# Last batch's queries and keys turned by DMA instead of TensorE, and MLP groups that choose their PSUM bank

## The chip, the cores and the metric

The kernel runs on one core of one Trainium2 chip. The time is device microseconds from the launch of the program to its end on that core. Before the change ten runs gave a median of 292.9 us (291.88 to 293.35).

## What is computed

Two blocks follow each other. The first is chunked attention with a few memory rows: 4 batches, 8 heads, 768 positions, 64 dimensions, chunks of 32 queries.

```python
for c in range(nc):                       # 24 chunks
    q_c   = q[:, :, 32*c : 32*c + 32]
    k_ctx = k[:, :, max(0, 32*c - 16) : min(768, 32*c + 40)]
    v_ctx = v[:, :, same range]
    a = softmax(q_c @ concat(mem_k, k_ctx).T / 8)      # 8 memory rows
    out[:, :, 32*c : 32*c + 32] = a @ concat(mem_v, v_ctx)
```

The second takes the heads side by side as x (4, 768, 512), mixes it with a Fourier transform along positions and along channels, and applies an MLP:

```python
u  = x + real(fft(fft(x, axis=1), axis=2))
un = (u - mean(u)) / sqrt(var(u) + 1e-6)
out = u + relu(un @ w_ch1) @ w_ch2                     # 512 -> 2048 -> 512
```

Inputs and output are float32.

## The kernel before

The work is 16 attention steps (n = 0 to 15; each is a pair of heads of one batch, four steps per batch), then for each batch a Fourier stage and an MLP.

**One attention step.** `e_load_qk` (L321) loads the pair's queries and keys with a cast to bf16, one DMA each on GpSimd's queue: 96 partitions, on each of them 8 neighbouring positions of both heads (tiles qs and ks, three of each). `e_load_v` (L327) issues seven DMAs on SP. `e_turn_q` and `e_turn_k` (L354, L363) transpose on TensorE, 16 small transposes each (`turn`, L347, line L351 in the profile), into a PSUM tile trq or trk. ScalarE copies trq into qT with positions in order (`e_qT`, L360) and trk into the windows of kTb (`e_kT`, L379; for batch 0 VectorE does that). `e_scores` (L392) makes the scores of six 64-query blocks, 12 matmuls of 64 columns, twice per step; `e_exp` (L400) takes exponents on ScalarE; `e_values` (L416) multiplies by the values in fp32; `e_norm` (L426, L427) divides on VectorE into xsb.

**Fourier and MLP of a batch.** VectorE folds xsb, splits it into fp16 halves (hi on ScalarE, lo on VectorE), TensorE makes the row transform (ps, L488; batch 0: L627, L614) and the column transform (pm, L638, L539). The lower half of the positions needs mirrored rows: `e_rows_out` (L522, GpSimd's queue) writes them to DRAM, `e_rows_turn` (L526, SP) reverses them there, `e_mirror` (L531, GpSimd's queue) reads them back as xr. VectorE adds (L644, L546, L548) and takes statistics (L652); ScalarE subtracts the mean into un (L658). For batches 1 to 3 un is transposed by a DMA on SP (`e_flip`, L670) into unT; for batch 0 by TensorE. The MLP runs in two halves of 384 positions: 16 groups `e_ch1` (ph, L698, four matmuls of 384 columns), each followed by a ReLU on ScalarE (`e_relu`, L706, hT), then three blocks of `e_ch2` (pc, L713, sixteen matmuls of 512 columns) and `e_osb` (L720) on VectorE.

**PSUM.** Two banks are tagged acc (Fourier results, and batch 0's key turns), two mlp, one each tr and xa, two sc. An MLP group's tag is fixed by its index:

```python
def mtag(b, i):
    return "acc" if i % 3 == 2 else "mlp"
```

**What sets the order.** Nothing is scheduled at run time: every engine runs its instructions in a written order. `Plan` (L37) makes that order once, before the program is built. Each task has an engine, a cost, tasks that it follows (`after`, `behind`), buffer slots that it takes and gives, and a rank; `Plan.order` (L90) walks through time, starts on each engine the task of lowest rank that is ready, and lists the tasks in order of their start. MLP tasks have the highest ranks on TensorE and so fill what is left between the others. While TensorE waits early in batch 0, the plan writes in matmuls on zeros (`e_fill`, L771, idle in the profile). DMAs get a time on a shared queue model (`share`).

At the start GpSimd clears edges and tiles (L296, L754, L777), and then issues the loads of step 3 (line L324 in the profile).

Of the kernel before, what the change touches and what calls it, by code (L numbers as in the profile page):

```python
# [36 lines left out]
class Plan:  # L37
# [11 lines left out]
    def __init__(self, slots):  # L49
        self.free = dict(slots)  # L50
        self.tasks = []

    def add(self, engine, cost, emit, after=(), take=(), give=(), rank=None, moved=0.0,
            loose=False, late=0.0, filler=False, behind=None, lag=0.0):
        t = dict(engine=engine, cost=cost, emit=emit, after=[a for a in after if a is not None],
                 take=take, give=give, rank=len(self.tasks) if rank is None else rank,
                 moved=moved, done=None, at=None, no=len(self.tasks), loose=loose,
                 late=late, filler=filler, behind=behind, lag=lag)
        self.tasks.append(t)
        return t  # L60
# [29 lines left out]
    def order(self):  # L90
        now, idle = 0.0, {}
        self.flow, self.seen = {}, 0.0
        waiting = {}
# [6 lines left out]
        while any(waiting.values()):  # L100
            for tag in [g for g in gives if g[0] <= now]:
                gives.remove(tag)
                self.free[tag[1]] += 1
            moved = False
            for e, ts_ in waiting.items():
                if idle.get(e, 0.0) > now:
                    continue
                held = False
                for t in ts_:
                    slack = (self.SLACK if e == "PE" and now > self.FIRST and not t["filler"]  # L110
                             else 0.0)
                    if held and not t["loose"]:
                        continue
                    if any(a["done"] is None
                           or (a["end"] > now if a["engine"] == e else a["done"] > now - slack - t["lag"])
                           for a in t["after"]):
                        held = held or (e == "SP" and not t["loose"])
                        continue
                    if t["behind"] is not None and t["behind"]["at"] is None:
                        continue  # L120
                    need = {}
                    for tag in t["take"]:
                        need[tag] = need.get(tag, 0) + 1
                    if any(self.free[tag] < m for tag, m in need.items()):
                        held = held or (e == "SP" and not t["loose"])
                        continue
                    for tag in t["take"]:
                        self.free[tag] -= 1
                    cost = t["cost"] * (2.0 if e == "PE" and now < self.WARM else 1.0)
                    idle[e] = t["end"] = now + cost  # L130
                    if t["moved"]:
                        self.flow.setdefault(e, []).append([t, t["moved"], now + cost])
                        self.share(now)
                        t["end"] = t["done"]
                    else:
                        t["done"] = now + cost + self.LAG.get(e, 0.07)
                    for tag in t["give"]:
                        gives.append((t["done"], tag))
                    t["at"] = now
                    placed.append(t)  # L140
                    ts_.remove(t)
                    moved = True
                    break
                else:
                    if e == "PE" and self.filling and self.filling[0]["at"] is not None \
                            and self.filling[1]["at"] is None:
                        cost = self.FILL * (2.0 if now < self.WARM else 1.0)
                        idle[e] = now + cost
                        placed.append(dict(engine="PE", cost=cost, emit=self.fill, at=now,
                                           done=now + cost))  # L150
                        moved = True
# [12 lines left out]
def kernel(  # L164
# [61 lines left out]
    NKT = 2  # L226
    kTb = [spool.tile([P, NT, P], BF16, name=f"kTb{i}") for i in range(NKT)]

    cp_q = "p h j d -> p h (j d)"
# [3 lines left out]
    plan = Plan(dict(qs=NS, ks=NS, va=NV, kTb=NKT, qT=2, tr=1, sc=1, xa=1, e1=3,  # L233
# [87 lines left out]
    def e_load_qk(n, i):  # L321
        b, pr = seq[n]
        src, dst = ((q, qs), (k, ks))[i]
        nc.gpsimd.dma_start(dst[n % NS][0:QP],  # L324
                            src[b, 2 * pr:2 * pr + 2].rearrange("h (p j) d -> p h (j d)", j=RB))
# [27 lines left out]

    def e_turn_q(n):  # L354
# [22 lines left out]
    def e_kT(n, eng=None):  # L377
        trk = tr_of.pop((n, 1))
# [6 lines left out]
    def e_scores(n, g):  # L385
        qT, kT = qT_of[n], kTb[n % NKT]
        sc_of[n, g] = sc = aps.tile([P, 2, 8, 64], FP32, tag="sc", bufs=1, name="sc")
        for t6 in range(6):
            t = 6 * g + t6
            for hh in range(2):  # L390
                r0 = 64 * hh
                nc.tensor.matmul(sc[:, hh, t6, :], kT[r0:r0 + 64, t, :],  # L392
                                 qT[r0:r0 + 64, ts(t, 64)], start=True, stop=True,
# [296 lines left out]
    def mtag(b, i):  # L690
        return "acc" if i % 3 == 2 else "mlp"
# [3 lines left out]
    def e_ch1(b, sh, ht):  # L695
        ph_of[b, sh, ht] = ph = bank(mtag(b, ht), [P, 512], FP32, "ph")
# [12 lines left out]
    def e_ch2(b, sh, stl, part):  # L709
        if part == 0:  # L710
            pc_of[b, sh, stl] = bank(mtag(b, stl), [P, DM], FP32, "pc")
# [95 lines left out]
    t_gate, LATE = None, 1.0  # L807

    def attention(n):
# [3 lines left out]
        lq, lk = [add("POOL", 0.9, lambda i=i: e_load_qk(n, i), take=(("qs", "ks")[i],),  # L813
                      moved=1.2, late=LATE if b else 0.0,
                      behind=t_gate if n == HP else t_ck.get(n - 1),
# [6 lines left out]
        if n == HP - 1:  # L822
            def e_gate():
# [3 lines left out]
        tq = add("PE", 0.40, lambda: e_turn_q(n), [lq, t_idb], take=("tr",), give=("qs",))  # L827
        dve = ("DVE", nc.vector.tensor_copy) if n < HP else ("ACT", None)
        eq = add("ACT", 0.80, lambda: e_qT(n), [tq], take=("qT",), give=("tr",),
                 rank=SINES - 0.5 if n == 0 else None)  # L830
        ktag = "acc" if first else "tr"
        tk = add("PE", 0.43, lambda: e_turn_k(n), [lk, t_idb, t_kz if n == 0 else t_kzs], take=(ktag,), give=("ks",))
        mk = t_mk[n] = add("DVE", 0.2, lambda: e_mkT(n), [t_mkT, t_kTz[n % NKT], t_mk.get(n - 1)],
                           take=("kTb",))
        ek = add(dve[0], 1.25 if dve[1] else 1.04, lambda: e_kT(n, dve[1]), [tk, mk], give=(ktag,))
# [157 lines left out]
    def columns_of(b, t_rest):  # L993
# [25 lines left out]
        for i, kt in enumerate(kts):  # L1019
# [14 lines left out]
            if b > 0:  # L1034
                t_un[kt] = add("SP", 0.1, lambda kt=kt: e_flip(b, kt),
                               [un, t_un.get(kts[i - 1]) if i else None],
                               take=("unT",) if i == 0 else (), give=("un",), moved=0.8,
# [11 lines left out]
    def mlp(b, t_un, rs):  # L1049
        for sh in range(2):  # L1050
            relu = []
            c2 = None
            for ht in range(NHT):
                ph = add("PE", 0.65, lambda sh=sh, ht=ht: e_ch1(b, sh, ht),
                         mlp_prev + [t_un[slot(b, 3 * sh + i)] for i in range(3)] + t_w1,
                         take=(mtag(b, ht),), give=("unT",) if sh == 1 and ht == NHT - 1 else (),
# [3 lines left out]
                                take=("hT",) if ht == 0 else (), give=(mtag(b, ht),),  # L1060
                                rank=RELU(len(plan.tasks))))
            for stl in range(3):
                st, end_b = slot(b, 3 * sh + stl), 3 * sh + stl == NST - 1
                for part in range(4):
                    end = part == 3
                    c2 = add("PE", 0.88, lambda sh=sh, stl=stl, part=part: e_ch2(b, sh, stl, part),
                             [relu[4 * part + 3], t_w2[part], c2], take=(mtag(b, stl),) if part == 0 else (),
# [4 lines left out]
                          give=(mtag(b, stl), "xsb") if end_b else (mtag(b, stl),),  # L1072
# [62 lines left out]
```

## Time and profile before

| | us |
|---|---|
| median of ten runs (lowest, highest) | 292.9 (291.88, 293.35) |
| the profiled execution, its own time | 291.95 |
| its span, first to last instruction | 290.2 |
| TensorE busy | 273.6 |
| VectorE busy / ScalarE busy | 164.6 / 164.6 |
| GpSimd busy | 48.2 |

The granted TensorE clock is 0.998 over the span. PE is TensorE, DVE VectorE, ACT ScalarE, POOL GpSimd, SP the engine that issues most DMAs. Matmuls are pipelined: a matmul's duration in the profile overlaps the next one's, so the cost of a group is read from start to start. The chain that ended last follows the program back from its last instruction, at each step to what released it.

| stretch (us) | PE busy | ACT busy | DVE busy | DMA GB/s |
|---|---|---|---|---|
| 0 to 10 | 2.45 | 6.87 | 8.44 | 131 |
| 22 to 40 | 18.00 of 18 | 9.91 | 17.34 | 190 |
| 100 to 120 | 20.00 of 20 | 15.27 | 13.78 | 145 |
| 120 to 140 | 20.00 of 20 | 16.07 | 14.62 | 172 |
| 200 to 220 | 19.11 of 20 | 10.03 | 9.82 | 66 |
| 260 to 280 | 20.00 of 20 | 7.84 | 2.25 | 66 |

### The profile page before, as it was taken

How to read it: one execution, taken by the hardware profiler on the slowest of the kernel's cores; microseconds unless marked ns; L12 is line 12 of the kernel's file. 1: busy time of each engine (PE TensorE's matmuls, PEld its weight loads, DVE VectorE, ACT ScalarE, POOL GpSimd, SP SyncE). 2: the span in 40 equal slices, each digit the busy share in tenths (PEclk: the TensorE clock that was granted, in tenths of full speed). 3: DMA queues.
4: the chain of work that ended last, by engine and by line, in shares of the span. 5: the costliest groups of instructions: out<-in, count | busy, mean ns of one | idle time of the engine just before them, and what ended most of it. 6: DMA issues, size and time to landing. Idle time of an engine off the chain costs nothing.

```text
span 290.2 us, 7349 instructions
## 1 busy us (share of the span) xinstructions
PE 273.6 (94%) x3055; PEld 172.6 (59%) x3055; DVE 164.6 (57%) x354; ACT 164.6 (57%) x294; POOL 48.2 (17%) x96
## 2 busy tenths in 40 slices
PE   1489998999999999999999999999899999999994
PEld 1377797765566766566677656656554645545541
DVE  7879998951269865948884978864912012012011
ACT  5897456768566586877884257433750721712700
POOL 8823922310321010221010021000020000000000
PEclk9999999999999999999999999999999999999999
DMA  6999999997999995899940366954222504004204
GB/s 104 200 188 161 206 210 196 196 198 146 193 201 267 165 258 69 137 134 230 164 100 29 38 145 183 147 145 111 54 54 82 101 10 125 13 36 108 38 36 108
DMA packets 98689, 38.36 MB, mean 132 GB/s; under 512 B 85728, under 2 KB 93920, under 8 KB 98656
## 3 DMA queue, kind: packets, MB, share of 16 engines
q1 hardware_dynamic: 87344, 21.83, 40.5%
q0 software_dynamic: 10592, 15.21, 27.6%
q10 hardware_dynamic: 720, 0.85, 0.9%
q8 instruction: 24, 0.39, 0.6%
q14 instruction: 9, 0.07, 0.1%
HBM read 37.36 MB, written 13.37 MB: 175 GB/s over the span
## 4 chain that ended last, share of the span: by engine, by line
PE 88%; DVE 4%; POOL 4%; ACT 2%; issue 1%; POOLq 0%; DVEq 0%
PE pc L713 29%; PE ph L698 29%; PE xa L416 8%; PE ps L488 5%; PE sc L392 3%; PE pm L638 3%; PE trk L351 2%; PE ps L627 2%; PE idle L771 2%; PE trq L351 2%; DVE st L652 1%; DVE xsb L644 1%; PE xo L416 1%; PE ps L614 1%; ACT e L400 1%
## 5 line engine op out<-in xcount | busy, mean ns | idle before, releaser
L706 ACT ACTIVATE hT<-ph 128x384 f16<-128x384 f32 x128 | 60.8, 492 | 53.0 <-PE ph L698 52.0
L698 PE MATMUL ph<-unT,w_sb 128*128 128x384 f16 x512 | 88.9, 326 | 0.9 <-ACT hT L706 0.6
L713 PE MATMUL pc<-w_sb,hT 128*128 128x512 f16 x384 | 88.0, 380 | 0.0
L698 PEld LDWEIGHTS <-w_sb 128*128 128x128 f16 x512 | 48.4, 98 | 33.2 <-issue 1.9
L713 PEld LDWEIGHTS <-hT 128*128 128x128 f16 x384 | 35.9, 98 | 40.6 <-issue 0.4
L720 DVE SCALAR_TENSOR_TENSOR osb<-pc,rstd,xsb 128x512 f32<-128x512 f32 x24 | 18.0, 750 | 72.4 <-PE pc L713 72.4
L400 ACT ACTIVATE e<-sc,mbias 128x384 f32<-128x384 f32 x64 | 33.6, 578 | 10.9 <-PE sc L392 9.3
L416 PEld LDWEIGHTS xa<-va,e 128*64 128x64 f32 x672 | 22.0, 137 | 6.8 <-issue 5.4
L416 PE MATMUL xa<-va,e 128*64 128x65 f32 x672 | 25.7, 226 | 0.0
L658 ACT ACTIVATE un<-xsb,mu_s 128x512 f16<-128x512 f32 x24 | 17.2, 722 | 14.2 <-DVE mu_s L653 14.2
L500 ACT CAST up<-ps 128x386 f16<-128x386 f32 x16 | 9.7, 605 | 16.9 <-PE ps L488 15.6
L652 DVE BATCH_NORM_STATS2 st<-xsb 128x6 f32<-128x512 f32 x24 | 16.6, 691 | 0.7
L360 ACT COPY qT<-trq 128x768 bf16<-128x768 bf16 x16 | 12.7, 795 | 6.8 <-PE trq L351 6.8
L324 POOL DMA_DIRECT2D qs<-in_q_dram x16 | 10.5, 659 | 35.7 <-PE trq L351 21.9
L427 DVE TENSOR_TENSOR xsb<-xa,zs 128x384 f32<-128x384 f32 x28 | 15.6, 558 | 1.0
L505 DVE TENSOR_TENSOR up<-ps,up 128x386 f16<-128x386 f32 x16 | 9.5, 595 | 10.7 <-ACT up L500 10.7
L351 PE MATMUL trq<-ident_b,qs 96*64 96x96 bf16 x256 | 9.1, 218 | 6.3 <-DMA qs<-in_q_dram 5.0
L426 DVE RECIPROCAL zs<-xa 128x6 f32<-128x6 f32 x28 | 5.4, 191 | 15.8 <-PE xa L416 15.4
L379 ACT COPY kTb<-trk 128x1056 bf16<-128x1056 bf16 x12 | 12.5, 1040 | 2.2 <-PE trk L351 2.2
L324 POOL DMA_DIRECT2D ks<-in_k_dram x16 | 10.2, 638 | 20.1 <-PE trk L351 16.0
L644 DVE TENSOR_TENSOR xsb<-pm,xsb 128x512 f32<-128x512 f32 x15 | 10.1, 670 | 5.4 <-PE pm L638 5.4
L392 PE MATMUL sc<-qT,kTb 64*128 64x64 bf16 x384 | 11.3, 193 | 1.6 <-ACT e L400 1.3
(142 smaller groups left out, 326.4 us busy)
## 6 DMA issues: line engine op xcount, KB each, us to landing
va<-in_v_dram SPq DMA_DIRECT2D x32, 220.0 KB
w_sb<-in_moe_w_ch_dram POOLq DMA_DIRECT2D x8, 512.0 KB, 16.7
qs<-in_q_dram POOLq DMA_DIRECT2D x16, 192.0 KB, 5.8
ks<-in_k_dram POOLq DMA_DIRECT2D x16, 192.0 KB, 5.6
out_dram<-osb SPq DMA_DIRECT2D x12, 256.0 KB
x_rows<-xsb POOLq DMA_DIRECT2D x3, 768.0 KB, 4.9
xr<-x_back POOLq DMA_DIRECT2D x3, 768.0 KB, 5.4
out_rows<-osb SPq DMA_DIRECT2D x9, 256.0 KB
```

The costliest lines, as they stand in the source:

```text
L324: nc.gpsimd.dma_start(dst[n % NS][0:QP], src[b, 2 * pr:2 * pr + 2].rearrange("h (p j) d -> p h (j d)", j=RB))
L351: nc.tensor.transpose(out_[64 * hh:64 * hh + 64, j * w:(j + 1) * w], src[:, hh, j * D:(j + 1) * D], eye)
L392: nc.tensor.matmul(sc[:, hh, t6, :], kT[r0:r0 + 64, t, :], qT[r0:r0 + 64, ts(t, 64)], start=True, stop=True, tile_position=(r0, 0))
L400: nc.scalar.activation(e1[:, :, :, ts(half, 32)], sc[:, :, 0:6, ts(half, 32)], AFT.Exp, bias=mbias[:, half:half + 1], scale=1.0 / math.sqr ...
L416: nc.tensor.matmul(xa[64 * half:64 * half + 64, st, hh, 0:65], e1[:, hh, t6, :], v1[:, hh, 6 * g + t6, 0:65], start=True, stop=True)
L427: nc.vector.tensor_tensor(xs[b][:, 3 * g:3 * g + 3, 2 * pr * D:(2 * pr + 2) * D] .rearrange("p s (h d) -> p s h d", h=2), xa[:, :, :, 0:D] ...
L652: nc.vector.bn_stats(st6, xs[b][:, kt, :])
L658: nc.scalar.activation(un, xs[b][:, kt, :], AFT.Identity, bias=mu_of[b][:, kt, 0:1], scale=-1.0)
L698: nc.tensor.matmul(ph[:, 0:384], w1_sb[:, dt, ts(ht, P)], unT_of[b][:, dt, sh * 384:(sh + 1) * 384], start=(dt == 0), stop=(dt == NDT - 1))
L706: nc.scalar.activation(hT_of[b, sh][:, ht, :], ph[:, 0:384], AFT.Relu, bias=0.0, scale=-1.0)
L713: nc.tensor.matmul(pc_of[b, sh, stl], hT_of[b, sh][:, ht, ts(stl, P)], w2_sb[:, ht, :], start=(ht == 0), stop=(ht == NHT - 1))
L720: nc.vector.scalar_tensor_tensor(osb, pc, rstd_of[b][:, st:st + 1], xs[b][:, st, :], ALU.mult, ALU.add)
```

## The change

For the last batch (steps 12 to 15; `TURNED = 3`) each load is split into two DMAs, one per head, that interleave the heads in 64-element pieces: [position in block][head][dimension]. Two DMA transposes on SP then put queries into qT as [2 x 64, 8, 96] and keys into the new tile kU. The queries are not copied further: the score matmuls read qT with a step of 96 elements. ScalarE copies the keys from kU into kTb. kU has two buffers, cleared once by GpSimd. The loads of step 12 are placed behind batch 1's `e_mirror`.

MLP groups no longer have a fixed tag: `pick` takes, when the group starts in the plan, that of the acc and mlp banks which has been free the longest (half a microsecond of preference for mlp). The planner's charge for all DMA transposes changes from a transfer on the queue model to 1.2 us of SP and 1.6 us until they land; this alters the order too.

```diff
 class Plan:
     def __init__(self, slots):
-        self.free = dict(slots)
+        self.free = dict(slots, **{"": 0})
...
     def order(self):
...
-        waiting = {}
+        waiting, since = {}, {}
...
                 self.free[tag[1]] += 1
+                since.setdefault(tag[1], []).append(tag[0])
...
-                    for tag in t["take"]:
+                    take = t["take"]
+                    if t["pick"] is not None:
+                        take += tuple(sorted((x for x in t["pick"]["of"] if self.free[x] > 0),
+                                             key=lambda x: (since.get(x, []) + [0.0])[0]
+                                             + t["pick"]["of"].index(x) * 0.5))[:1] or ("",)
+                    for tag in take:
                         need[tag] = need.get(tag, 0) + 1
...
-                        t["done"] = now + cost + self.LAG.get(e, 0.07)
+                        t["done"] = now + cost + (t["late"] or self.LAG.get(e, 0.07))
+                        if e == "SP":
+                            t["end"] = t["done"]
...
+    KR, KS, NKU = 16, 128, 2
+    kU = [spool.tile([P, RB, KS], BF16, name=f"kU{i}") for i in range(NKU)]
+    TURNED = 3
...
     def e_load_qk(n, i):
         b, pr = seq[n]
         src, dst = ((q, qs), (k, ks))[i]
+        if b >= TURNED:
+            for hh in range(2):
+                nc.gpsimd.dma_start(
+                    dst[n % NS][0:QP].rearrange("p h (j d) -> p (h j) d", d=D)[:, hh::2],
+                    src[b, 2 * pr + hh].rearrange("(p j) d -> p j d", j=RB))
+            return
...
+    def e_flip_q(n):
+        qT_of[n] = qT = apool.tile([P, RB, QP], BF16, tag="qT", bufs=2, name="qT")
+        nc.sync.dma_start_transpose(qT, qs[n % NS].rearrange("p h c -> p (h c)"))
+
+    def e_flip_k(n):
+        nc.sync.dma_start_transpose(kU[n % NKU][:, :, KR:KR + QP],
+                                    ks[n % NS][0:QP].rearrange("p h c -> p (h c)"))
...
     def e_kT(n, eng=None):
+        if n >= TURNED * HP:
+            nc.scalar.copy(
+                strided(kTb[n % NKT], MEM0 + NMEM, [[P, NT], [RB, 11], [1, RB]]),
+                strided(kU[n % NKU], KR - KOFF, [[64 // RB, NT], [1, 11], [KS, RB]]))
+            return
...
     def e_scores(n, g):
...
-                nc.tensor.matmul(sc[:, hh, t6, :], kT[r0:r0 + 64, t, :],
-                                 qT[r0:r0 + 64, ts(t, 64)], start=True, stop=True,
+                own = (qT[r0:r0 + 64, ts(t, 64)] if n < TURNED * HP else
+                       strided(qT[r0:r0 + 64], t * 64 // RB, [[1, 64 // RB], [QP, RB]]))
+                nc.tensor.matmul(sc[:, hh, t6, :], kT[r0:r0 + 64, t, :], own, start=True, stop=True,
                                  tile_position=(r0, 0))
...
-    def mtag(b, i):
-        return "acc" if i % 3 == 2 else "mlp"
+    pick_of = {}
+
+    def pick(*key):
+        return pick_of.setdefault(key, dict(of=("mlp", "acc")))
...
     def e_ch1(b, sh, ht):
-        ph_of[b, sh, ht] = ph = bank(mtag(b, ht), [P, 512], FP32, "ph")
+        ph_of[b, sh, ht] = ph = bank(pick(b, sh, ht)["tag"], [P, 512], FP32, "ph")
...
+    t_uz = add("POOL", 0.4, lambda: [nc.gpsimd.memset(kU[i], 0.0) for i in range(NKU)], rank=20)
...
-        lq, lk = [add("POOL", 0.9, lambda i=i: e_load_qk(n, i), take=(("qs", "ks")[i],),
-                      moved=1.2, late=LATE if b else 0.0,
-                      behind=t_gate if n == HP else t_ck.get(n - 1),
+        lq, lk = [add("POOL", 1.6 if b >= TURNED else 0.9, lambda i=i: e_load_qk(n, i),
+                      take=(("qs", "ks")[i],), moved=3.1 if b >= TURNED else 1.2, late=LATE if b else 0.0,
+                      behind=t_gate if n == HP else t_xr[b - 2] if n == TURNED * HP else t_ck.get(n - 1),
...
+        if b >= TURNED:
+            eq = add("SP", 1.2, lambda: e_flip_q(n), [lq], take=("qT",), give=("qs",),
+                     late=1.6, loose=True, behind=t_flip[0])
+            t_flip[0] = tk = add("SP", 1.2, lambda: e_flip_k(n), [lk, t_uz], take=("kU",),
+                                 give=("ks",), late=1.6, loose=True, behind=eq)
+            ek = add("ACT", 2.05, lambda: e_kT(n), [tk, mk], give=("kU",))
+        else:
...
...
-                t_un[kt] = add("SP", 0.1, lambda kt=kt: e_flip(b, kt),
-                               [un, t_un.get(kts[i - 1]) if i else None],
-                               take=("unT",) if i == 0 else (), give=("un",), moved=0.8,
+                t_un[kt] = add("SP", 1.2, lambda kt=kt: e_flip(b, kt),
+                               [un], behind=t_un.get(kts[i - 1]) if i else None,
+                               take=("unT",) if i == 0 else (), give=("un",), late=1.6,
                                loose=True)
...
                 ph = add("PE", 0.65, lambda sh=sh, ht=ht: e_ch1(b, sh, ht),
-                         take=(mtag(b, ht),), ...
+                         pick=pick(b, sh, ht), ...
```

## The prediction

> **What bounds the kernel now.** I read the page's busy table and slices first, then the chain that ended last, then the chain over three short windows, then the group rows that price the edited operations.
>
> ```profile
> span 290.2 us, 7349 instructions
> PE 273.6 (94%) x3055; PEld 172.6 (59%) x3055; DVE 164.6 (57%) x354; ACT 164.6 (57%) x294; POOL 48.2 (17%) x96
> PE   1489998999999999999999999999899999999994
> PE 88%; DVE 4%; POOL 4%; ACT 2%; issue 1%; POOLq 0%; DVEq 0%
> ```
>
> TensorE (PE) is idle in the first three slices and the last; between, it is full, and 88% of the chain that ended last is PE. From about 53 us to 286 us the end therefore moves by what PE is given to do, plus what PE must wait. The windows confirm it: 20.00 of 20 us busy in every 20 us stretch from 60 to 280, except 200 to 220 (19.11). The turns that the change removes lie on that chain:
>
> ```profile
> 118.70 0.28 PE sc L392 x12
> 118.98 0.46 PE trq L351 x16
> 119.44 1.83 PE pc L713 x8
> 121.28 0.28 PE sc L392 x12
> 121.56 0.47 PE trk L351 x16
> 122.03 3.56 PE pc L713 x16
> ```
>
> Columns: start, length on the chain, what. Sixteen small transposes cost PE 0.46 us, and MLP matmuls stand on both sides, so nothing hides them. Twelve score matmuls cost 0.28 us (23.5 ns each).
>
> Before 53 us the kernel is not PE-bound but a relay between engines, and one transfer in it is just in time (timeline; start, duration, engine, line):
>
> ```profile
> 15.86 0.63 POOL L324 DMA_DIRECT2D ks<-in_k_dram  x1
> 21.18 0.51 PE L351 MATMUL trq<-ident_b,qs 96*64 96x96 bf16 x16
> 21.52 0.53 PE L351 MATMUL trk<-turn_b,ks 100*64 100x100 bf16 x16
> 21.97 0.35 PE L392 MATMUL sc<-qT,kTb 64*128 64x64 bf16 x12
> ```
>
> This is pair 3's key load. The view of the tile ks gives 5.5 us from issue to landing, so it lands at 21.4 us, and PE turns it at 21.52: 0.16 us of slack.
>
> **The change, part by part** (line numbers of before).
>
> *Turns removed.* For n = 12 to 15, e_turn_q and e_turn_k go: eight sets of 16. Start to start in PE's timeline they take 0.47, 0.47, 0.37 (a values group follows), 0.47, 0.47, 0.48, 0.46 and 0.38 us, 3.57 in all. Where MLP work stands on both sides, the switch ahead of a turn costs a further 0.1 us (ph x8 takes 1.41 before query turn 15, against 8 x 0.1625 = 1.30 in the pure runs at the end). Sum **-3.7 us**, all on the path.
>
> *Bank choice (pick).* It replaces mtag, by which every third MLP group had to have an acc bank. The waits view shows what that cost:
>
> ```profile
> PE ph L698 <- ACT hT L706: 0.6, 1, 0.6
> PE ph L698 <- DVE xsb L548: 0.3, 1, 0.3
> ```
>
> Both lie between 206.4 and 208 us: an MLP group waits for an acc bank that VectorE has still to empty of a Fourier result. They are the only MLP waits of PE. Bounds 0 and -0.9; I take **-0.6**, since another group may then be first to wait.
>
> *The new memsets.* kU is two tiles of 128 x 1024 bf16, cleared on GpSimd. Comparing the instruction orders, they stand immediately ahead of pair 3's query and key loads, and the planner charges 0.4 us. The rows say otherwise:
>
> ```profile
> L754 POOL MEMSET ks<- 4x1024 bf16 x2 | 2.0, 1026 | 0.0
> L777 POOL MEMSET kTb<- 128x384 bf16 x2 | 0.8, 423 | 0.1
> ```
>
> 1.0 to 1.1 ns per element of a partition row, whatever the number of partitions: 2 x 1.03 = 2.05 us. The key load is issued at 17.9, lands at 23.4, and PE stands at its turn 2.05 - 0.16 = 1.9 us longer. PE's order there is fixed (the idle matmuls of L771 are written in, not elastic), the scores, exponents, values and norms of pairs 2 and 3 stand behind it, and VectorE, 17.3 of 18 us busy from 22 to 40, waits for each of those norms. So the shift reaches 53 us whole and stays. Bounds: 0, if the transfer lands no later because fewer v packets compete then, to 2.05; I take **+1.9**.
>
> *Scores with a strided moving operand.* qT for n >= 12 is laid out as [j, 96], so the 64 query columns of a score matmul are read 96 elements apart. No row of before has a strided bf16 moving operand. Lower bound 0: the 23.5 ns of the L392 row hold, since they are already less than streaming needs alone (ph streams 384 columns in 162.5 ns, so 64 take 27 ns) and the two row halves evidently overlap. Upper bound, the slowest moving stream of similar length in the trace, the fp32 values group: 24 records of 65 columns in 0.85 us, two records to a matmul, 70.8 ns: 96 x (70.8 - 23.5) = +4.5 us. I take one such record, 35.4 ns, the row nearest to the present one: 96 x 11.9 ns = **+1.1 us**.
>
> [...]
>
> *ScalarE.* Four qT copies of 0.80 us go (-3.2). The four kT copies now read SBUF with a stride instead of PSUM: 1.04 us (L379) at least; the planner charges 2.05, no row shows it: 0 to +4.0 us. ScalarE is busy 43.2 of 58 us from 87 to 145, so this hides in its gaps; if they were gone, scores would wait for kTb. Counted at 0.
>
> *Loads.* Eight cast loads become 16, 768 pieces of 256 bytes each instead of 192 of 2 KB. GpSimd issue: 0.64 us at 192 pieces and 0.83 at 384 (L522) extrapolate to 1.2 us, 19 us in all on an engine 17% busy. Packets: 12,288 new ones at the 21.5 ns of the hardware queue's mean (40.5% of 16 engines, 87,344 packets of 250 bytes) are 16.5 us of all engines, against 1,536 x 121 ns / 16 = 11.6 us of the software queue's now: +5 us over some 35 us in which the DMA digits read 5 to 9. The loads of n = 12 and 13, issued from 82 to 91 us now, move behind batch 1's mirror load (102 us). Behind them on POOL stand batch 1's rstd (123 us, first needed past 150) and batch 2's row store.
>
> *Transposes on SP.*
>
> ```profile
> L670 SPq DMA_TRANSPOSE unT<-un x18: 1188/1213/1306, 115.5 to 214.6; - x18
> ```
>
> Eight more, of 1.5 times the elements: 1.2 to 1.8 us of SP each. Each waits for its load, and on SP stand behind it the v loads of n = 14 and 15 (3.7 to 5 us of issue each) and batch 1's own transposes. Now the flip that completes batch 1's first three MLP blocks starts at 121.4 us and PE needs it at 132.6. In the new order it stands behind both transposes of n = 13, which wait for loads that start after 102 us, and behind v of n = 14: 115.5 + 1.2 + 4.4 + 5 x 1.2 to 1.5 puts it at 127 to 129, while PE, rid of six turns, arrives near 129.8. The 11 us of cover shrink to about 1. Cost 0 to +2.5 us; I take **+0.3**.
>
> Sum: -3.7 - 0.6 + 1.9 + 1.1 + 0.3 = **-1.0 us**. The profiled execution took 291.95 us (span 290.2 and 1.75 around it), among the fastest of ten; it would become 290.95. The median is 292.9, so the forecast is 291.9. A difference under 0.2% (0.6 us) can't be told from none.
>
> **The rivals.**
>
> *B, slower: the strided query read.* Place: the eight score groups of batch 3, on a full PE. The other terms sum to -2.1 us, so it decides from 22 ns more per matmul (45 ns). At half the streaming rate of the ph row, 54 ns, the result is 293.7; at the fp32 price of 70.8 ns, 295.3. For it: 96-element steps. Against it: the two halves overlap, so 54 ns of stream may show as 27. Chance 0.21.
>
> *C, slower: late data.* The small pieces or the longer SP queue make PE wait at the first ph of batch 1, at the scores of n = 12 or 13, or ScalarE at kT, which holds un and so the MLP input. It decides from 1.6 us more than I counted; 2.5 us beyond my sum gives 294.4. For it: cover of 11 us down to 1. Against it: loads land in 3.4 to 6 us at present. Chance 0.13.
>
> *D, nothing measurable:* memset and stride eat the turns, 292.3 to 293.5. Chance 0.14.
>
> *E, the full gain:* the key load lands in time after all and the scores keep 23.5 ns: -3.7 - 0.9 + 0.3 + some 0.8 of memset = -3.5, 289.4. Chance 0.12.
>
> **How the numbers follow.** The forecast has 0.40, its own range 290.9 to 292.3. Faster is 0.40 + 0.12 = 0.52, same 0.14, slower 0.21 + 0.13 = 0.34. The range runs from E's 289.4 to B's upper price, 295.3; about 0.06 lie above and as much below.
>
> **What would show it.** No trq or trk after 120 us, and eight sets fewer. PE idle of some 1.9 us at pair 3's trk near 21 to 23 us, released by the ks load, after two kU memsets of about 1 us. Scores of n >= 12: 12 starts over 0.28 us (E), about 0.4 us (mine) or 0.65 us and more (B). No PE wait for xsb L548 near 206 us. PE waits on unT or kTb between 120 and 145 us would be C. I am wrong if PE's idle before 53 us is unchanged, or if its busy sum from 53 us on shrinks by less than 2 us.

## The result, and the profile after

The changed kernel takes **295.58 us** (median of 15 runs, 293.31 to 298.64); the kernel before 293.09 us (52 runs, 291.5 to 296.17). The ratio is **1.0081, 95% interval 1.006 to 1.0101**: slower by some 2.4 us, where the forecast was 1.0 us faster. The profiled execution took 295.39 us (span 293.7), 3.5 us of span more than before. Medians are of all executions, but ratios leave out those over 1.5% above the fastest of their kernel (most in e9, four of twelve, and e13, five of twelve), and the profiles used of e2, e6, e9, e12 and e13 are of such executions.

The page of after, busy times, TensorE's slices and the shares of the chain that ended last:

```profile
span 293.7 us, 7118 instructions
PE 275.5 (94%) x2927; PEld 172.9 (59%) x2927; DVE 165.6 (56%) x354; ACT 166.2 (57%) x290; POOL 57.0 (19%) x106
PE   1589998998999999999999999999999999999994
PE 78%; DMA 5%; POOL 5%; DVE 4%; ACT 3%; SPq 2%; issue 2%; POOLq 0%; DVEq 0%
```

128 matmul instructions fewer than before ran on PE, yet it is busy for 1.9 us more: work was taken away and as much came back. PE's share of the chain fell from 88% to 78%, and "DMA" and "SPq", which had none, have 7%: at some places the end now waits for transfers.

Where the removed work came back, in the timeline (start, duration, engine, line; times in brackets are PE's idle time and its releaser):

```profile
123.62 0.35 PE L428 MATMUL sc<-qT,kTb 64*128 64x64 bf16 x12
128.65 0.82 PE L428 MATMUL sc<-qT,kTb 64*128 64x64 bf16 x12 [0.16 <-ACT e L435]
129.41 2.76 PE L750 MATMUL pc<-w_sb,hT 128*128 128x512 f16 x12
132.10 0.82 PE L428 MATMUL sc<-qT,kTb 64*128 64x64 bf16 x12
```

A pair is the pair of heads of one step, with the step's number. The first row is pair 11 (old layout), the second and fourth pair 12. From the first start of a group to what follows, 0.28 us became 0.76: 63 ns for a matmul instead of 23.5. That is 12 x 39.5 ns = 0.475 us a group and, for eight groups, **+3.8 us**, all of the 3.7 us that the eight removed turns brought.

The start, in the timelines of GpSimd and PE:

```profile
15.10 1.85 POOL L845 MEMSET kU<- 128x1024 bf16 x2
17.52 0.63 POOL L345 DMA_DIRECT2D ks<-in_k_dram  x1
21.58 0.53 PE L372 MATMUL trq<-ident_b,qs 96*64 96x96 bf16 x16 [0.64 <-DMA qs<-in_q_dram]
22.73 0.54 PE L372 MATMUL trk<-turn_b,ks 100*64 100x100 bf16 x16 [0.62 <-DMA ks<-in_k_dram]
```

Pair 3's key load is issued 1.66 us later than before and PE turns it 1.21 us later. And the waits of PE (total, times, longest), with the window where before idled, of before and of after (its us, then us and instructions of PE, PEld, DVE, ACT and POOL, clock, DMA share, GB/s):

```profile
PE xa L451 <- DMA va<-in_mem_v_dram: 1.4, 1, 1.4
PE ph L735 <- DMA unT<-un: 0.4, 1, 0.4
```

```profile
200.00:220.00 20.00, 19.11 (x116) 10.86 (x114) 9.82 (x22) 10.03 (x21) 1.60 (x2) 1.00 0.28 66
200.00:220.00 20.00, 20.00 (x134) 12.37 (x132) 10.89 (x24) 12.25 (x24) 1.60 (x2) 1.00 0.29 68
```

The 1.4 us are new: at 68.6 us pair 6's first values group stands in the middle, waiting for its v load. The 0.4 us are batch 1's MLP waiting for its last transposes. In 200 to 220 us PE is busy for 20.00 us instead of 19.11: the bank waits are gone. One profile against the other: -3.7 (turns) - 0.9 (banks) + 3.8 (strided reads) + 1.2 (start) + 1.4 (v load) + 0.4 (unT) + 0.5 (an "issue" gap ahead of a trk, no releaser shown) = +2.7 of the 3.5 us; 0.8 us I can't assign. This profile was granted a clock of 1.000; eleven of the fifteen runs had 0.994 or less (see the last section).

### The profile page after: what moved, and what is told of

It is laid out like the page before. It is cut to its first block, busy times and chain, and to the rows that moved or that the text cites. A ratio compares the mean times of both kernels' runs of the same rounds, so it can differ in the third digit from the quotient of the medians.

```text
span 293.7 us, 7118 instructions
## 1 busy us (share of the span) xinstructions
PE 275.5 (94%) x2927; PEld 172.9 (59%) x2927; DVE 165.6 (56%) x354; ACT 166.2 (57%) x290; POOL 57.0 (19%) x106
## 3 DMA queue, kind: packets, MB, share of 16 engines
q0 software_dynamic: 21472, 15.21, 31.7%
## 4 chain that ended last, share of the span: by engine, by line
PE 78%; DMA 5%; POOL 5%; DVE 4%; ACT 3%; SPq 2%; issue 2%; POOLq 0%; DVEq 0%
PE ph L735 26%; PE pc L750 26%; PE xa L451 6%; PE ps L523 5%; PE pm L673 3%; PE sc L428 3%; DMA va<-in_mem_v_dram 3%; PE ps L662 2%; SPq L354 2%; DMA ks<-in_k_dram 2%; PE idle L808 2%; DVE st L687 1%; PE trk L372 1%; PE trq L372 1%; DVE xsb L679 1%
## 5 line engine op out<-in xcount | busy, mean ns | idle before, releaser
L743 ACT ACTIVATE hT<-ph 128x384 f16<-128x384 f32 x128 | 61.6, 490 | 55.9 <-PE ph L735 54.9
L451 PE MATMUL xa<-va,e 128*64 128x65 f32 x672 | 26.5, 229 | 1.4 <-DMA va<-in_mem_v_dram 1.4
L451 PEld LDWEIGHTS xa<-va,e 128*64 128x64 f32 x672 | 22.6, 140 | 8.4 <-issue 5.6
L428 PE MATMUL sc<-qT,kTb 64*128 64x64 bf16 x384 | 15.2, 217 | 1.2 <-ACT e L435 1.2
L428 PEld LDWEIGHTS <-kTb 64*128 64x128 bf16 x384 | 10.4, 99 | 8.2 <-issue 6.0
L513 DVE TENSOR_TENSOR lo<-ff,hi 128x768 f16<-128x768 f32 x12 | 11.4, 955 | 3.9 <-ACT hi L508 3.6
L372 PE MATMUL trq<-ident_b,qs 96*64 96x96 bf16 x192 | 7.0, 221 | 6.3 <-DMA qs<-in_q_dram 6.3
L345 POOL DMA_DIRECT2D qs<-in_q_dram x12 | 8.0, 667 | 22.4 <-PE trq L372 17.5
L389 ACT COPY qT<-trq 128x768 bf16<-128x768 bf16 x12 | 9.6, 796 | 4.6 <-PE trq L372 4.6
```

Of the source, the lines that this page charges most:

```text
L428: nc.tensor.matmul(sc[:, hh, t6, :], kT[r0:r0 + 64, t, :], own, start=True, stop=True, tile_position=(r0, 0))
L451: nc.tensor.matmul(xa[64 * half:64 * half + 64, st, hh, 0:65], e1[:, hh, t6, :], v1[:, hh, 6 * g + t6, 0:65], start=True, stop=True)
L743: nc.scalar.activation(hT_of[b, sh][:, ht, :], ph[:, 0:384], AFT.Relu, bias=0.0, scale=-1.0)
```

## The experiments

Three lines of thought had to be told apart: the strided read ate the turns' gain (T); the transfers, smaller and later, are what holds the end (late data); and what the choice of bank does. Ratios are against before, with 95% intervals.

**1. Contiguous reads** (e1_contig). After, with

```
-  strided(qT[r0:r0 + 64], t * 64 // RB, [[1, 64 // RB], [QP, RB]])
+  qT[r0:r0 + 64].rearrange("p j a -> p (j a)")[:, ts(t, 64)]
```

> The score matmuls of the last batch read 64 neighbouring columns of qT instead of 8 x 8 columns with a step of 96; so they pair keys with the wrong queries, and everything else stays, with the same order on every engine. Theory (the strided read costs the 3.7 us that the removed turns brought): the eight score groups of n = 12 to 15 take 0.28 us instead of 0.75, 8 x 0.47 = 3.8 us, and the time falls from about 295.4 to 291.6 us, 0.995 to 1.000 of before. Rival (late data: the small pieces and SP's transposes are what holds the end, and the score groups lie in their shadow): the groups get shorter, but TensorE waits as much longer for qT, kTb or unT, and the time stays within 0.5 us of 295.4, about 1.008 of before.

Measured: 292.16 us median (12 runs), ratio 0.9944 (0.991 to 0.9978). Against after's 1.0081 that is 1.37% of before, 4.0 us: theory T. One access pattern turns this change from slower to faster (by less than 1%). Not all of the 4.0 us need be the reads' own time: among executions granted a clock of 0.997 or more the medians are 294.0 us (four of after's fifteen) and 291.2 (eight of twelve here), 2.8 us apart. The profile of e1 has no wait for va (PE reached that group at 67.8 us and went on), so the 1.4 us vary from run to run. And the rival is not empty: PE, no longer slowed, now waits longer for batch 1's transposes than after's 0.4 us.

```profile
125.84 0.35 PE L428 MATMUL sc<-qT,kTb 64*128 64x64 bf16 x12 [0.17 <-ACT e L435]
132.11 1.46 PE L735 MATMUL ph<-unT,w_sb 128*128 128x384 f16 x8 [1.12 <-DMA unT<-un]
```

**2. What the step costs** (e5_steps). After, pairs 12 to 15 read with other steps:

```
+  [[QP, 8], [1, 8]] if n == 12 else [[(1, 2, 4, 8)[n - 12], 64]]
```

> The query columns of the last batch's score matmuls are read with other steps, one for each pair, so they pair wrong queries: n = 12 in runs of 8 neighbouring columns with 96 between the runs, n = 13 every 2nd column, n = 14 every 4th, n = 15 every 8th (4, 8 and 16 bytes). A group of 12 takes 0.28 us with neighbouring columns and 0.75 with the step of 96. [...] Rival (a price for any step other than 1): 0.75 for n = 13 to 15 alike. Second rival (the price comes only with steps far above 16 bytes): 0.28 for n = 13 and 14 at least.

One row for each of pairs 12, 13, 14 and 15, in PE's timeline:

```profile
130.75 0.35 PE L428 MATMUL sc<-qT,kTb 64*128 64x64 bf16 x12
140.72 0.35 PE L428 MATMUL sc<-qT,kTb 64*128 64x64 bf16 x12
155.93 0.52 PE L428 MATMUL sc<-qT,kTb 64*128 64x64 bf16 x12
166.12 0.85 PE L428 MATMUL sc<-qT,kTb 64*128 64x64 bf16 x12
```

A group has these lengths with contiguous reads: 0.35; with the step of 96: 0.82. So runs of 8 neighbours 192 bytes apart cost nothing, every second column (4 bytes) nothing, every fourth (8 bytes) 0.17 us, every eighth (16 bytes) 0.50, no less than the 0.47 of the step of 96 (192 bytes). Both rivals fail: a price for any step at 4 and 8 bytes, a price only far above 16 bytes at 8 and 16. Why the price comes between 4 and 16 bytes and is no higher at 192, these lengths don't show.

**3. The other axis order** (e10_out_turned). After, read in runs of 8, written with a step:

```
-  strided(qT[r0:r0 + 64], t * 64 // RB, [[1, 64 // RB], [QP, RB]])
+  strided(qT[r0:r0 + 64], t * 64 // RB, [[QP, RB], [1, 64 // RB]])
+  to = strided(sc[:, hh, t6, :], 0, [[1, RB], [RB, 64 // RB]])
```

> After with the two axes of the strided read swapped: a score matmul of the last batch reads 8 runs of 8 neighbouring query columns, and its output is written with a step of 8 fp32 columns, so each score lands where it did. All else as in after. Theory (the price is on the side of the read, by the step of the innermost columns: 0.35 us for 12 matmuls in runs of 8, 0.82 with the step of 96): groups of 0.35 us, 295.4 - 3.8 = 291.6, about 0.994 of before like the contiguous version. Rival (a step on the output costs as much as one on the read): groups of 0.8 us, 1.008 of before.

Measured: 293.97 us, 1.0027 (0.9995 to 1.006). Between the theories: a group takes 0.51 us instead of 0.35 or 0.82.

```profile
125.93 0.51 PE L429 MATMUL sc<-qT,kTb 64*128 64x64 bf16 x12
```

The step on the output costs a third of that on the read, 8 x 0.16 = 1.3 us, and the ratio stands 0.8% above the contiguous version, about 1 us more than that accounts for.

**4. The clears later** (e2_kU_late). After, with

```
+  t_uz["behind"] = t_ck[2 * HP]     # behind the loads of batch 2's first pair
```

> The two clears of kU on GpSimd move from the first 17 us to behind the query and key loads of batch 2's first pair; nothing else changes place on any engine. Theory (the clears hold pair 3's key load, and that shift lasts to the end): pair 3's key load is issued near 15.7 instead of 17.5 us, trk of pair 3 starts near 21.5 instead of 22.7, and the time falls by 1.2 us, to about 294.2 (1.004 of before). Rival (slack taken up later: a later wait ends at the same time whatever happened at 22 us): trk moves all the same, but a wait at 68 to 70 us or later grows by as much, and the time falls by less than 0.4 us.

Measured: 296.51 us, 1.0095 (1.0057 to 1.0132), no gain. Pair 3's key load is issued at 15.97 us and its trk starts at 21.74 instead of 22.73, as the theory says; but PE then waits longer, for pair 6's v load and for an exponential (PE's waits):

```profile
PE xa L451 <- DMA va<-in_mem_v_dram: 2.6, 1, 2.6
PE sc L428 <- ACT e L435: 5.5, 2, 4.7
```

1.4 us became 2.6: in this profile what was won at 22 us was given back at 68, as the rival says. In the four profiles with this wait (after, e2, e4, e6) PE comes to the group at 67.6 to 68.6 us and goes on at 69.99, 70.23, 70.40 and 70.93; in e1's the load was there by 67.8. The second line is late data: ScalarE waits 6.0 us for pair 12's key transpose before it can copy kT, and PE 4.68 us behind it. The profile of e9 (experiment 6), which also clears late, has the same wait, 4.6 us.

**5. The choice of bank** (e3_no_pick and e4_pick_only). The first is after with `mtag` back, the second before with `pick` alone.

> After with the fixed bank names of before (every third group on acc, the others on mlp); turns by DMA, clears and strided reads stay. Theory (the choice of bank saves the 0.9 us of bank waits near 206 us, but its order also puts pair 6's first values group ahead of the v load, which costs 1.4 us at 68.6 to 70): the wait for va goes, the bank waits come back, 295.4 - 1.4 + 0.9 = 294.9 us, about 1.006 of before. Rival (the wait for va is not from the order but from the transfers' times, and stays without the choice): 295.4 + 0.9 = 296.3 us, about 1.011 of before.

> Before with the choice of bank alone: no DMA turns, no clears. It takes pair 6's first values group 12 chunk matmuls forward, as in after. Theory (the choice saves the bank waits of 0.9 us near 206 us and costs a wait for pair 6's v load at 68 us, which varies with the transfers from 0 to 3 us): 291.95 - 0.9 + (0 to 3), about 292.5 us, 0.997 to 1.004 of before. Rival (the choice is worth here what it was worth in after, where fixed names cost 1.1%): 292.0 - 3.3 = 288.7, about 0.989 of before.

Measured: without the choice 298.36 us, 1.0194 (1.0138 to 1.0249); the choice alone 295.71 us, 1.0088 (1.006 to 1.0116). Both ratios lie outside every interval stated. Without the choice the wait for va is gone, as its theory says, but PE waits 2.8 us for banks in all (1.4, 0.6, 0.5 and 0.3 by its waits) where before lost 0.9, in the order that the DMA turns bring; so in after the choice is worth 1.1%. Alone it costs 0.9%, for it changes more than banks: in its order three MLP groups (12 matmuls) fewer stand ahead of pair 6's first values group, which so comes to the v load too early. PE in the choice alone:

```profile
67.32 0.34 PE L426 MATMUL xa<-va,e 128*64 128x65 f32 x4
70.40 0.80 PE L426 MATMUL xa<-va,e 128*64 128x65 f32 x20 [2.75 <-DMA va<-in_mem_v_dram]
```

**6. Values of pair 6 placed later** (e11_pick_v, e9_kU_late_v). The planner is told a later landing for that one load, which moves the two values groups on PE and nothing else:

```
-  take=("va",), moved=2.7, late=LATE if b else 0.0)
+  take=("va",), moved=2.7, late=26.6 if n == 6 else LATE if b else 0.0)
```

> Before with the choice of bank alone, and pair 6's two values groups 3.5 and 3 us later on TensorE. Theory (all that the choice alone costs is the wait for pair 6's v load, 2.7 us in its profile, and it saves the bank waits near 206 us): 294.5 - 2.7 = 291.8 or 291.1 with the second part, 0.995 to 1.000 of before. Rival (the choice costs elsewhere too): above 1.003.

> After with the clears of kU moved to batch 2 and pair 6's two values groups placed 3.5 and 3 us later on TensorE; strided reads stay. Theory (the 1.2 us that the clears cost at 22 us were given back to the wait for pair 6's v load, 2.6 us with the clears late against 1.4): with both, 295.4 - 1.2 - 1.4 = 292.8 us, about 0.9995 of before (0.996 to 1.003). Rival (both are taken up again by the late un transposes near 134 us): 294.5 or more, above 1.004.

Measured: before with choice and later values 291.43 us, **0.9941** (0.9918 to 0.9965), and all 12 runs within 290.60 to 291.89; after with late clears and later values 294.09 us, 0.9999 (0.9962 to 1.0036). The first is slightly better than its theory's interval, the second lies in its own. From 1.0088 to 0.9941 are 4.3 us for moving two groups of 0.85 us each; the profiles, both at a clock of 1.000, differ by 3.6 us of span, 2.75 of it the wait. Nine of the eleven executions of the choice alone were granted 0.994 or less, all twelve with the later values 0.997 or more, so the wait mostly goes with a lowered clock as well. And from 1.0081 to 0.9999 are 2.4 us for the clears and the wait together, where 2.6 was expected. This run doesn't separate the two: the later values alone were worth 4.3 us in the other kernel, so what the clears cost at the end stays open.

**7. A layout without strides** (e6_fix, e7_fix_v). Positions in blocks of 128, so that the transposes leave them in order; the second has the later values too:

```
-  dst[0:QP]... [:, hh::2],  src[...].rearrange("(p j) d -> p j d", j=RB)
+  dst...       [:, hh:2*NST:2],  src[...].rearrange("(c p) d -> p c d", p=P)
-  memset(kU[i], 0.0)                       # 2 x 1024 columns
+  memset(kU[i][:, c:c + KR], 0.0) for c in (0, KR + S)   # 4 x 16 columns
```

> The last batch's queries and keys are loaded by 128 consecutive positions to 128 partitions in 6 blocks, heads side by side (again 768 pieces of 256 bytes an issue), so that the same DMA transposes leave qT and kU in order of position: scores read 64 neighbouring columns, the kT copy runs of 88, and only 16 columns at each end of kU have to be cleared (4 clears of 16 columns instead of 2 of 1024). The order on every engine stays. Theory: 3.8 us less from the scores and 1.0 to 1.2 less from the clears, 295.4 - 4.9 = 290.5 us, 0.988 to 0.995 of before; the kT copy falls from 2.05 to about 1 us off the path. Rival (late data): the loads have the same number of pieces and the transposes the same place, so the time stays at 294 to 295.4.

> The last batch in blocks of 128 positions (contiguous reads, short clears) as before, and pair 6's two values groups stand 3.5 and 3 us later on TensorE, behind work that is ready; no other instruction changes place on any engine. Theory (what held the contiguous version at 289 to 294.8 us is pair 6's v load, which TensorE waits for by 3.0 us in its profile, and after which the granted clock is 0.50 for 3 us): no wait for va between 66 and 75 us, no clock below 1.0 there, profile near 289, the runs within 3 us of each other, ratio 0.984 to 0.990. Rival (the wait only moves, to the next group that needs a transfer): ratio 0.990 as it was.

Measured: 290.99 us, 0.990 (0.9851 to 0.9948), and 291.12 us, 0.9917 (0.9885 to 0.9949). The first is as expected. The later values removed the wait at 68 us (PE is busy for 20.00 of 20 us from 60 to 80, against 16.96) but not the spread: runs from 289.49 to 294.36. It goes with the clock: six executions granted 0.997 or more took 289.5 to 291.5 us, six granted 0.994 or less 291.0 to 294.4. So the rival of the second holds as far as the time goes, and it raised the question of the last group: the turns take 3.7 us off PE, but this median is only 0.3 us below that of e11, which leaves the turns on PE. In e7's profile PE waits 1.5 us for unT at 131 us.

**8. Why the data are late** (e12_fix_flips, e13_fix_no_pick, e14_act_flips, e15_big_pieces, e16_two_pairs). All start from the layout of 7; all but e13 have the later values. e12 tells the planner that a query or key transpose lands after 4.0 us instead of 1.6; e13 has the fixed bank names; e14 issues those transposes from ScalarE's queue (`nc.scalar.dma_start_transpose`); e16 turns only pairs 14 and 15 by DMA (`n >= TURNED * HP + 2`); e15 loads in large pieces:

```
-  dst ... [:, hh:2 * NST:2],        src[...].rearrange("(c p) d -> p c d", p=P)
+  dst ... [:, ts(hh, NST * D)],     src[...].rearrange("(p c) d -> p (c d)", p=P)
```

> The version in blocks of 128 positions with values 6 later, and the scheduler told that a query or key transpose lands 4.0 us after SP takes it (1.6 before; the trace showed 3.7 from its issue to the kT copy). On ScalarE this puts pair 13's kT copy behind two normalisations of batch 1's MLP input and one exponential, instead of in front of them; nothing else moves but one output store on SP. Theory (the 1.5 us that TensorE waits for unT at 131 us are the kT copy's wait of 3.0 us for kU, with the normalisations queued behind it): the un transposes are issued 2 us earlier, the wait for unT goes, 291.1 - 1.5 = 289.6, 0.983 to 0.989 of before. Rival (the un transposes are held by SP's own queue, by the q transpose and the loads ahead of them): the wait stays, 0.992.

> The version in blocks of 128 positions with the fixed bank names of before: the DMA turns without strided reads, without long clears and without the choice of bank; pair 6's values groups stand where before has them. Theory (fixed names cost 2.8 us of bank waits in the order that the DMA turns bring, as in the profile of after without the choice): 298.4 - 3.8 - 1.2 = 293.4, 1.000 to 1.006 of before, with bank waits between 160 and 220 us. Rival (with the reads and clears mended the order's bank waits are the 0.9 us of before, and the turns' 3.7 us show): 290 or less, 0.990.

> The version in blocks of 128 positions with values 6 later, and the last batch's query and key transposes issued from ScalarE's queue instead of SP's; the scheduler places them there, which moves some other work too. Theory Q (the un transposes are late because they stand behind the query and key transposes and their waits on SP's queue): the wait for unT near 131 us goes (1.5 us in the profile without this), 0.985 of before. Theory D (the DMA engines themselves are full between 105 and 130 us, 1.4 to 2.4 by the DMA share against 0.7 to 1.4 with the turns on TensorE, so every transfer there is late whichever queue issues it): a wait of 1 to 6 us for unT, or for the exponential behind the kT copy, stays near 125 to 137 us, 0.990 or more.

> The version in blocks of 128 positions with values 6 later, but the last batch's loads read 1536 bytes in a row for each partition and head instead of 6 pieces of 256: 128 pieces an issue instead of 768, the same bytes, issues and order on every engine. The scores are then of mixed heads and positions. Theory D (the many small pieces fill the DMA engines): the DMA share between 105 and 130 us falls from 1.4 to 2.4 to the 0.7 to 1.4 of the kernel with TensorE turns, loads land in 4 us or less instead of 7 to 8, the wait for unT near 131 us falls to 0.3 or less, and the time to 288.5 to 290, 0.983 to 0.988 of before, with runs within 2 us of each other. Theory Q (SP's queue): share or not, the wait for unT stays over 1 us, 0.990.

> As the version in blocks of 128 positions with values 6 later, but only the last two pairs (14 and 15) are turned by DMA; pairs 12 and 13 are loaded and turned on TensorE as before. Theory D (the loads of small pieces and the transposes collide with batch 1's v loads and un transposes between 105 and 130 us; those of pairs 14 and 15 come when there is less to collide with): half of the 3.7 us of turns comes back on the path, 1.8, no wait for unT over 0.5 us near 131, and the runs lie within 3 us: 291.4 - 1.8 = 289.6, 0.984 to 0.990 of before. Rival (the collision moves with them to the un transposes of batch 2 near 150 to 165 us): 0.994 or more.

e12: 293.59 us, 0.9987 (0.9949 to 1.0024), worse. The kT copy did move and the two normalisations did run first, but the un transposes did not go earlier. In SP's timeline and PE's:

```profile
123.98 3.39 SPq L377 DMA_TRANSPOSE qT<-qs  x1
127.47 2.60 SPq L705 DMA_TRANSPOSE unT<-un  x2
136.81 2.72 PE L735 MATMUL ph<-unT,w_sb 128*128 128x384 f16 x8 [6.53 <-DMA unT<-un]
```

A query transpose of 1.2 us at its shortest held SP for 3.39, with those of un behind it: the rival. e13: 295.09 us, 1.0006 (0.9967 to 1.0045), in the theory's interval, with bank waits of 1.1, 0.6, 0.5 and 0.5 us between 168 and 213 us; its profile also waits 2.7 us for unT. Against e7 the choice is worth about 1% in this layout too. e14: 303.65 us, 1.0355 (1.0319 to 1.039). It decides nothing between Q and D: SP issued nothing from 109.8 to 123.6 us and the first un transpose only at 132.3, though ScalarE had normalised it by 117.5, and the trace shows no releaser; PE waited 11.9 us for unT.

e15 settles what the pieces cost: **288.11 us, 0.9836** (0.9804 to 0.9869), 287.51 to 289.3, the fastest of all. Its issues stand in the same order as e7's and move the same bytes; only the pieces differ. The windows from 105 to 130 us (PE, PEld, DVE, ACT, POOL busy; clock; DMA share; GB/s) of before, e7 and e15:

```profile
105.00:130.00 25.00, 25.00 (x368) 16.20 (x366) 14.99 (x34) 18.86 (x32) 4.15 (x6) 1.00 0.80 143
```

```profile
105.00:130.00 25.00, 24.22 (x308) 14.46 (x305) 16.52 (x38) 16.03 (x29) 11.30 (x14) 1.00 1.77 176
```

```profile
105.00:130.00 25.00, 25.00 (x324) 15.23 (x323) 16.74 (x39) 17.40 (x30) 6.38 (x11) 1.00 1.16 173
```

At nearly equal GB/s (176 and 173) the DMA engines are half as busy again with the pieces of 256 bytes (1.77 against 1.16). From 100 to 140 us the software queue (GpSimd's) moved 3.15 MB in both, in 12960 packets that took 76.6% of all engines' time in e7 and in 2720 that took 41.2% in e15, 14.2 us of all engines less. With large pieces the q loads land in 5.8 us instead of 7.9 (median of 100 to 140 us, issue to landing; four or less was expected), and PE waits for unT nowhere. An issue also took GpSimd less, 0.53 instead of 0.82 us, which this run can't separate from the pieces' time on the DMA engines. Nor does it rule out SP's queue as the way by which the delay reaches PE: in the order that both share un's transposes stand behind those of queries and keys (in e7 those of un start at 124.43 and 129.66 us, behind a query transpose at 122.66 and a key transpose at 128.34). e15's scores are of mixed heads, so it is a measure of the pieces, not a version to keep; a head-by-head layout needs pieces of 256 bytes.

e16 has the lowest median of the versions whose scores are of the right heads and positions: 290.02 us, **0.9906** (0.9872 to 0.994), 289.11 to 292.85, a little above the 0.984 to 0.990 that were expected. No wait for unT, PE full from 60 to 220 us, share 1.24: half of the turns, at a quieter place. By the intervals it can't be told from e7 or e6; it beats both kernels of this case by about 1% or more, as do those two, and e11 with no DMA turn at all is 0.6% below before.

## Why the prediction was wrong, step by step

- **Turns removed, -3.7 on the path: right.** PE was full on both sides. The contiguous versions show the gain, less what late data take.
- **Strided reads, +1.1: the step that failed.** It cost 3.8 us, 63 ns a matmul. The bounds (0 to 4.5) held it, but the value was taken at one fp32 record, 35.4 ns, "the row nearest to the present one", on the thought that two row halves overlap and hide it. A contiguous bf16 row says nothing on a stride. Taken at rival B's 54 ns, an estimate (half the streaming rate of the ph row) that no run shows, the stride costs 96 x 30.5 ns = 2.9 us, the sum is +0.8 us and its sign right; the runs showed 63 ns. Rival B (0.21) is what happened: with 3.8 us in this place and every other term as it stood the forecast is 294.6. The 1.0 us from there to the 295.58 is what the other terms come to by the profiles: the v load +1.4, the issue gap +0.5, late data +0.1, clears -0.7, banks -0.3.
- **Clears, +1.9: right in kind, too large in size, and not shown to last.** The two clears took 1.85 us (2.05 forecast) and PE was 1.21 us late at trk. The shift did reach 53 us whole (a score group at 57.03 against 55.80); that it "stays" isn't shown, for without it PE waited as much longer at 68 us (experiment 4), and experiment 6 moved the values as well.
- **Bank choice, -0.6: right where it looked, wrong in its bounds.** The waits near 206 us went, -0.9. But 0 to -0.9 excluded a loss, and the choice is also a change of order; alone it costs 0.9%. The wait for va was in no term and in no rival, though the orders of the instructions show the values group coming forward, and SP's timeline of before has pairs of v issues that take 4 to 11 us between 35 and 70 us.
- **Late data, +0.3: right in after's profile (0.4), by luck.** The strided read made PE late and so hid it. Without that read PE waits 1.1 us (e1) to 1.5 us (e7), and large pieces bring 2.4 us (0.9917 to 0.9836). Rival C named the place; its cause was the pieces, which the packet count had priced at 5 us of all engines and then set aside. By the queue tables of the two pages the software queue took 13 us more of all engines (27.6% of 290.2 us, then 31.7% of 293.7), and the hardware queue, with the eight transposes that the packet count left out, another 12 (40.5%, then 44.0%).
- **kT copy, 0 on the path: right.** It took 2.05 us a copy, 1.07 with runs of 88, and neither shows on PE's path by itself.
- **The issue cost of the loads**, extrapolated to 1.2 us, was 0.77 in after and 0.82 in e7.
- **The tests.** No trq or trk ran after 120 us, the clears and the wait for ks stood where they should, and 0.76 us for 12 starts is rival B's range. The test for being wrong fired: PE's busy sum from 53 us on, which should have shrunk by 2 us or more, grew from 232.2 to 233.9 (by 0.8 us when counted from the same score group, at 55.80 and 57.03).

## What to carry to other kernels

When a layout change removes an instruction, price the reads that the new layout leaves, at full price until a row shows otherwise: a moving operand of bf16 columns 192 bytes apart cost 2.7 times as much here (63 ns a matmul instead of 23.5), and that ate the whole gain. A new choice of resources in a planner is a new order: look at what comes forward and which transfer it needs, and whether a saving upstream only lengthens that wait. Count DMA in pieces as well as bytes (the same bytes in 128 pieces an issue instead of 768 took the ratio from 0.9917 to 0.9836 here), and expect a cost that a slow step hides to appear when the step is mended.

## What the runs showed of the hardware

- **A wait can cost more than its length.** In the profile of e6, PE waits 3.04 us for va from 67.9 us (window, PE busy, ..., granted clock, DMA share, GB/s):

```profile
69.00:70.00 1.00, 0.00 (x0) 0.00 (x0) 0.00 (x0) 0.00 (x0) 0.00 (x0) 1.00 1.11 242
71.00:72.00 1.00, 1.00 (x20) 1.00 (x20) 0.00 (x0) 0.00 (x0) 0.00 (x0) 0.50 0.21 45
72.00:73.00 1.00, 1.00 (x9) 0.53 (x6) 0.64 (x2) 0.00 (x0) 0.00 (x0) 0.50 0.31 70
74.00:75.00 1.00, 1.00 (x7) 0.46 (x5) 0.00 (x0) 0.69 (x2) 0.00 (x0) 1.00 0.48 113
```

  The clock is halved for about 3 us; by that 1.5 us more are lost, an estimate. Waits of 1.36 us (after), 2.59 (e2) and 2.75 (e4) left it at 1.00; 2.74 (e13) halved it; and in e5 it was halved from about 23.8 to 27.2 us (0.90, 0.50, 0.50, 0.50 and 0.89 by the us from 23 to 28), where PE's waits since 18 us were 0.17, 1.01 and 0.73 us. Over whole executions the clock goes with the time: after's four at 0.999 or more have a median of 294.0 us, its eleven at 0.994 or less 295.9, while of before's 35 that stand beside e11 only six had 0.994 or less. So part of the slowdown of 2.4 us is likely clock; where the executions without a profile lost it isn't known. The length of a wait alone doesn't tell whether the clock is halved, for 2.74 us did it and 2.75 did not; what else does, as in e5, these runs don't show.
- **The strided matmuls didn't slow down at half clock.** In e2's profile a group of 12 took 0.83 us at a clock of 0.50 (132.7 us) and 0.82 at 1.00 (138.2): their length did not follow TensorE's clock. A contiguous group takes 0.50 us at half clock (e13, 134.7 us) and 0.35 at full.
- **ScalarE paid for a stride in SBUF too**: 1056 bf16 columns from SBUF in 2.05 us with a step of 256 bytes (after), 1.07 in runs of 88 (e6, e7), 1.04 from PSUM with a step (before).
- **GpSimd's clears took longer with more columns**: 0.96 us for 1024 columns of bf16 on 128 partitions, 0.42 for 384 (both in after).
